# Two integers spread over the partitions by a stream shuffle instead of a matmul, and one row of 17 dummies

## Chip, cores and metric

One core of a Trainium2 chip. The time is device microseconds (us) from the start of the program to its end, the median of several runs. A few microseconds at the start of the program are what the change touches; the span of the whole is over 600 us.

## What is computed

Attention with a band and a few global keys, then two feed-forward layers. `n_global` and `n_local` are 64-bit integers that are known only at run time.

```python
def _attn_ref(q, k, v, n_global, n_local):          # q, k, v: 2 x 8 x 768 x 64
    scores = scale * np.matmul(q, k.transpose(0, 1, 3, 2))
    rel = pos[:, None] - pos[None, :]
    is_global = pos[None, :] < int(n_global)
    is_local = (rel >= 0) & (rel < int(n_local))
    keep = is_global | is_local
    dist = np.where(is_global & ~is_local, float(n_local), np.abs(rel))
    scores = np.where(keep, scores - slopes[:, None, None] * dist, -1e9)
    a = np.exp(scores - np.max(scores, axis=-1, keepdims=True))
    a = a / (np.sum(a, axis=-1, keepdims=True) + 1e-09)
    return np.matmul(a, v)

def reference(...):
    x = attention, as 1536 x 512
    h = x @ w1_in;  x = np.maximum(0.01 * h, h) @ w1_out          # 512 -> 2048 -> 512
    h = x @ w2_in;  return (P(h) / (Q(h) + 1e-06)) @ w2_out       # polynomials in h
```

## The kernel before

The program has three stages: attention for 8 pairs of heads (up to about 100 us), then the first and the second feed-forward layer, all bound by TensorE (PE). Products of large tiles are made of three passes over a high and a low part of each operand (`qh`, `ql`, `kh`, `kl`). Each engine runs its instructions in the order in which the code issues them; the order was written out by hand, with tables such as `BUSY`, `PREP` and `DECS` that say after which unit of work a piece goes out. The lines outside the hand-ordered part, the loading of the two integers among them, may be moved on their queue by the compiler of the program.

The start, with which the change deals, runs so:

- ACT's DMA queue loads the two integers into one partition of the tile `ints` (L95, L96), and after them one half of the first k block (`kr`, L300). SP's queue loads the rest: q's first half for both heads of pair 0, k's first half of the other head, then the second halves, then k, v and q of pair 1.
- VectorE (DVE) fills the tile `warm` with ones. PE then multiplies `warm` by itself into the tile `idle`: these are the dummies of `keep_busy(n)` (L489), whose result nobody reads. `BUSY = (14, 1, 3, 2, 1, 2)` is how many stand at each of six places.
- GpSimd (POOL) makes the identity (`ident`), and index tables with iotas; DVE makes the distances from them (`misc`, L236, L237, L239) and turns the integers into floats (`read_ints`, L106 to L109), which gives two numbers in one partition (`num1`).
- After 14 dummies, PE multiplies a row of ones by `num1` (L500), which puts the two numbers into all 128 partitions of a PSUM tile (`spread`), and then does one more dummy. DVE copies them to `nums` (L509).
- From `nums`, DVE makes the mask (L245, L248) and the first part of the bias (L251). The distances in `misc` and the bias are kept for the whole attention.
- Meanwhile PE transposes q's first half and k's first half (L331). ScalarE (ACT) rounds them to `qh` (L370) and `kh` (L341), and DVE makes the rests `ql` (L372) and `kl` (L343), on its queue behind L251. Then PE multiplies `kh` by `qh`, and, after a few dummies, `kl` by `qh` and `kh` by `ql` (L402).

From the products with `kl` on, PE has nearly always something to do. What later pieces need of q, k and v comes by SP's queue, 96 KB or 192 KB at a time in packets of 256 bytes.

Of the kernel before, what the change touches and what calls it, by code (L numbers as in the profile page):

```python
# [8 lines left out]
F32 = mybir.dt.float32  # L9
F32R = mybir.dt.float32r  # L10
I32 = mybir.dt.int32
U32 = mybir.dt.uint32
AF = mybir.ActivationFunctionType
ALU = mybir.AluOpType
# [3 lines left out]
P = 128  # L18
# [8 lines left out]
def attention_moe_moe2(  # L27
# [15 lines left out]
    nc = tc.nc  # L43
# [17 lines left out]
    LOAD_Q = 5  # L61
    XOUT = (8, 9)

    BUSY = (14, 1, 3, 2, 1, 2)

    FIRST = 8
    XOUT_LAST = (1, 8)
# [17 lines left out]
    RUN_AHEAD = 2  # L85

    W2 = 2 * P
    BW = W2 + P

    cpool = ctx.enter_context(tc.tile_pool(name="cpool", bufs=1))  # L90
    xpool = ctx.enter_context(tc.tile_pool(name="xpool", bufs=1))


    ints = cpool.tile([1, 4], I32, name="ints")
    nc.scalar.dma_start(ints[:, 0:2], n_local.bitcast(I32).partition_broadcast(1))  # L95
    nc.scalar.dma_start(ints[:, 2:4], n_global.bitcast(I32).partition_broadcast(1))  # L96
    intf = cpool.tile([1, 4], F32, name="intf")
    num1 = cpool.tile([1, 2], F32, name="num1")
    warm = cpool.tile([P, P], F32R, name="warm")
    ones = warm.bitcast(F32)[0:1]  # L100
    nums = cpool.tile([P, 2], F32, name="nums")
    n_loc = nums[:, 0:1]
    n_glo = nums[:, 1:2]

    def read_ints():
        nc.vector.tensor_copy(intf, ints)  # L106
        lo, hi = (intf.rearrange("p (j w) -> p j w", w=2)[:, :, w] for w in range(2))
        nc.vector.scalar_tensor_tensor(hi, lo, 0.0, hi, ALU.is_lt, ALU.add)
        nc.vector.scalar_tensor_tensor(num1, hi, 4294967296.0, lo, ALU.mult, ALU.add)  # L109

    coef = cpool.tile([P, 8], F32, name="coef")

# [110 lines left out]
    def window_bias(bpool, rpool):  # L223
# [6 lines left out]
        mask = misc2[:, 0:BW]  # L230
        nc.gpsimd.iota(rel_i[:, 0:W2], [[-1, W2]], base=P, channel_multiplier=1)
        nc.gpsimd.iota(rel_i[:, W2:BW], [[-1, P]], base=0, channel_multiplier=1)
        col_i = bpool.tile([P, GW], I32, name="col_i")
# [10 lines left out]
        def far():  # L244
            nc.vector.tensor_scalar(mask, dist, n_loc, FAR, ALU.is_ge, ALU.mult)  # L245
            mask_g = misc2[:, 0 : 2 * W2].rearrange("p (a c) -> p a c", a=2)[:, :, 0:GW]
            col_g = col.unsqueeze(1).to_broadcast([P, 2, GW])
# [10 lines left out]
    def attention(wpool, w1, ffn):  # L258
        with ExitStack() as actx:
# [4 lines left out]
            ps = actx.enter_context(tc.tile_pool(name="ps", bufs=2, space=PSUM))  # L264
# [4 lines left out]
            def blocks(t, s):  # L269

                if s == 0:
                    return t[:, 0 : HB * W2].rearrange("p (i c) -> p i c", c=W2)[:, :, 0:P]
                c0 = HB * W2 - P
# [213 lines left out]
            def keep_busy(n, rows=P):  # L487
                for _ in range(n):
                    nc.tensor.matmul(  # L489
                        idle[:, 0:W2].rearrange("p (a c) -> p a c", a=2),  # L490
                        warm[0:rows],
                        warm[0:rows].unsqueeze(1).to_broadcast([rows, 2, P]),
                        start=True,
                        stop=True,
                    )

            bias, bias_far, bias_near, bias_half = window_bias(bpool, rpool)
            keep_busy(BUSY[0])
            spread = ps.tile([P, W2], F32, tag="pt", name="spread")[:, 0:2]
            nc.tensor.matmul(spread, ones, num1, start=True, stop=True)  # L500
            keep_busy(BUSY[1])
            q0, k0, q1, k1 = P_[0].prep_q(0), P_[0].prep_k(0), P_[0].prep_q(1), P_[0].prep_k(1)
            next(q0)
            next(k0)
            next(q0)
            next(k0)
            keep_busy(BUSY[2])
            own, rest = slice(W2, BW), slice(0, W2)
            nc.vector.tensor_copy(nums, spread)  # L509
            bias_far()  # L510
            bias_near(own)
            next(q0, None)
# [102 lines left out]
            while n < len(U) or running or n <= len(U) + LV + 1:  # L615

                for m in GROUPS.get(n, ()):
                    for step, _ in enumerate(zip(unit(m).scores(), unit(m + 1).scores())):
                        if n == 0 and step == 0:
                            keep_busy(BUSY[3], P // 2)  # L620
                    if m == 2:
                        for _ in zip(unit(4).scores(), unit(5).scores()):
                            pass
                        keep_busy(BUSY[4])
                for m in LEASTS.get(n, ()):
                    unit(m).least()
                    if m == 1:
                        bias_near(rest)
                        bias_half(rest)
                if unit(n - 1) and n != 3:  # L630
                    unit(n - 1).exp()
                if unit(n - 3):
                    unit(n - 3).transposes()
                    if n == 4:
                        keep_busy(BUSY[5], P // 2)
                    unit(n - 3).evacuate()
                if n == 3:
                    unit(2).exp()
                for m in {LV: (), LV + 1: (0, 1)}.get(n, (n - LV,)):
                    if unit(m):  # L640
                        unit(m).values()
                if unit(n - LV - 1) and unit(n - LV - 1).ih == HB - 1 and unit(n - LV - 1).j == 1:
                    unit(n - LV - 1).finish()
                fillers(n)
                n += 1
# [516 lines left out]
```

## Time and profile before

| | us |
|---|---|
| median of 3 runs | 634.55 (634.18 to 634.83) |
| the profiled execution, its time | 633.84 |
| its span | 632.1 |
| PE busy in the span | 625.4 (99%) |
| DVE, ACT, POOL busy | 468.5, 437.0, 208.7 |

The span is the time from the first to the last instruction of the trace; the 1.7 us between it and the profiled execution's time lie around it. In the chain of work that ended last, 99% of the span is PE's. To read such a kernel: where PE is always busy, its instructions follow each other and their sum is the time; only where PE waits can another engine's work change the end. PE's idle time is in the first microseconds and at the end. The page's column for the granted clock shows the full level in every slice; for the very start, the durations of the dummies have to be looked at beside it.

### The profile page before, as it was taken

The page shows a single profiled execution, that of the slowest core. Times are in us where ns is not written, and L with a number is a line of the kernel's source. Part 1 is how long each engine was busy: PE and PEld are TensorE (multiplying, and loading weights), DVE is VectorE, ACT ScalarE, POOL GpSimd, SP SyncE. Part 2 cuts the span into 40 slices and gives each one's busy share as a digit, 9 for nine tenths or more (in the row PEclk, how much of TensorE's full clock was granted, in tenths as well). Part 3 has the DMA queues.
Part 4 walks back from the last instruction along what each step waited for, and adds up shares of the span by engine and source line. Part 5 has one row for each costly group of instructions (what it writes and reads, how often), then busy time and mean ns, then how long its engine had stood idle before and what let it go on. Part 6 is the DMA issues. An engine that isn't in the chain of part 4 may idle for free.

```text
span 632.1 us, 9657 instructions
## 1 busy us (share of the span) xinstructions
PE 625.4 (99%) x3289; PEld 527.2 (83%) x3289; DVE 468.5 (74%) x931; ACT 437.0 (69%) x828; POOL 208.7 (33%) x223
## 2 busy tenths in 40 slices
PE   9999999999999999999999999999999999999996
PEld 7999998888888888888888888888888888888885
DVE  7889887878887555456444489998777777897785
ACT  5899997868866455455344477876677888876673
POOL 4888864534443334341000012222222222112220
PEclk9999999999999999999999999999999999999999
DMA  9998643854367776764332200000033331100002
GB/s 190 225 181 177 153 114 109 278 197 167 99 194 236 225 242 195 238 194 177 100 100 94 92 16 34 1 1 1 0 104 97 100 95 46 63 33 0 2 1 73
DMA packets 80895, 73.34 MB, mean 116 GB/s; under 512 B 50948, under 2 KB 67332, under 8 KB 80836
## 3 DMA queue, kind: packets, MB, share of 16 engines
q1 hardware_dynamic: 79920, 71.09, 39.5%
q0 software_dynamic: 224, 0.92, 0.4%
q8 instruction: 28, 0.46, 0.3%
q10 hardware_dynamic: 692, 0.62, 0.3%
q14 instruction: 31, 0.25, 0.1%
HBM read 60.69 MB, written 11.93 MB: 115 GB/s over the span
## 4 chain that ended last, share of the span: by engine, by line
PE 99%; DVE 0%; issue 0%
PE h L675 41%; PE y L798 21%; PE y L796 21%; PE pt L438 4%; PE sc L402 3%; PE o L460 3%; PE o L459 2%; PE h L331 2%; PE h L211 1%; PE idle L489 1%; PE o L457 0%; DVE ot L814 0%; PE xt L211 0%; PE spread L500 0%; DVE kl L343 0%; DVE ql L372 0%
## 5 line engine op out<-in xcount | busy, mean ns | idle before, releaser
L675 PE MATMUL h<-xh,w 128*128 128x512 f32 x768 | 253.5, 390 | 0.0
L675 PEld LDWEIGHTS h<-xh,w 128*128 128x128 f32 x768 | 144.3, 188 | 29.8
L675 PE MATMUL h<-xl,w 128*128 128x512 f32 x384 | 149.6, 389 | 0.0
L731 POOL TENSOR_TENSOR gl<-u,gh 128x512 fp32r<-128x512 f32 x44 | 57.1, 1298 | 264.6 <-PE y L798 125.6
L796 PE MATMUL y<-gh,w 128*128 128x512 f32 x384 | 126.1, 389 | 0.0
L798 PE MATMUL y<-w,gh 128*128 128x512 f32 x384 | 125.7, 390 | 0.0
L166 POOL TENSOR_TENSOR dec<-dec,wraw 128x512 int32<-128x512 int32 x48 | 64.1, 1344 | 82.5 <-DVE wraw L153 79.2
L798 PEld LDWEIGHTS y<-w,gh 128*128 128x128 f32 x384 | 72.0, 188 | 15.1 <-ACT gh L910 0.3
L796 PEld LDWEIGHTS y<-gh,w 128*128 128x128 f32 x384 | 72.1, 188 | 15.0
L675 PEld LDWEIGHTS h<-xl,w 128*128 128x128 f32 x384 | 72.1, 188 | 14.5
L798 PE MATMUL y<-w,gl 128*128 128x512 f32 x192 | 75.1, 391 | 0.0
L796 PE MATMUL y<-gl,w 128*128 128x512 f32 x192 | 74.7, 389 | 0.0
L700 DVE TENSOR_TENSOR gl<-h,gh 128x512 fp32r<-128x512 f32 x48 | 33.0, 688 | 52.4 <-ACT gh L699 52.4
L699 ACT ACTIVATE gh<-h 128x512 fp32r<-128x512 f32 x48 | 28.6, 596 | 59.7 <-PE y L796 56.4
L750 ACT ACTIVATE h<-h 128x512 f32<-128x512 f32 x48 | 28.7, 597 | 52.8 <-PE h L675 52.6
L695 DVE SCALAR_TENSOR_TENSOR h<-h,g 128x512 f32<-128x512 f32 x48 | 33.3, 694 | 25.8 <-ACT g L694 25.7
L737 DVE SCALAR_TENSOR_TENSOR w<-w,epsq,h 128x512 f32<-128x512 f32 (+1 forms) x49 | 36.6, 747 | 20.6 <-ACT h L761 19.9
L694 ACT ACTIVATE g<-h 128x512 f32<-128x512 f32 x48 | 28.7, 598 | 29.8 <-PE h L675 29.8
L752 DVE SCALAR_TENSOR_TENSOR w<-h,coef,w 128x512 f32<-128x512 f32 x48 | 36.0, 749 | 16.1 <-ACT w L751 16.0
L427 ACT ACTIVATE pr<-sn,st 128x256 f32<-128x256 f32 (+1 forms) x96 | 47.1, 495 | 0.2 <-DVE st L413 0.2
L798 PEld LDWEIGHTS y<-w,gl 128*128 128x128 f32 x192 | 36.1, 188 | 8.5 <-POOL gl L731 1.1
L796 PEld LDWEIGHTS y<-gl,w 128*128 128x128 f32 x192 | 36.0, 188 | 7.4
(124 smaller groups left out, 1117.3 us busy)
## 6 DMA issues: line engine op xcount, KB each, us to landing
wraw<-in_moe_w_in_dram SPq DMA_DIRECT2D x24, 512.0 KB, 4.5
wraw<-in_moe_w_out_dram SPq DMA_DIRECT2D x24, 512.0 KB, 4.8
scratch<-dec SPq DMA_DIRECT2D x32, 256.0 KB, 5.5
wf<-scratch SPq DMA_DIRECT2D x16, 512.0 KB, 3.5
w<-in_moe_w_in_dram SPq DMA_DIRECT2D x8, 512.0 KB, 4.4
w<-in_moe_w_out_dram SPq DMA_DIRECT2D x8, 512.0 KB, 5.3
vc<-in_v_dram SPq DMA_DIRECT2D x16, 192.0 KB, 3.4
qkraw<-in_q_dram SPq DMA_DIRECT2D x6, 512.0 KB, 3.5
```

Source lines behind the costliest of these rows:

```text
L166: nc.gpsimd.tensor_tensor(ti, ti, self.c, ALU.add)
L427: nc.scalar.activation(self.pr[:, :w], self.sn[:, :w], AF.Exp, bias=self.least_at, scale=-1.0,)
L675: nc.tensor.matmul(h, wt[:, m, c * P : (c + 1) * P], xs[:, c, cs], start=c == 0 and n == 0, stop=c == NK - 1 and n == 2,)
L694: nc.scalar.activation(g, h, AF.Copy)
L695: nc.vector.scalar_tensor_tensor(h, h, 0.01, g, ALU.mult, ALU.max)
L700: nc.vector.tensor_tensor(gl, h, gh.bitcast(F32), ALU.subtract)
L731: (nc.gpsimd if on_pool else nc.vector).tensor_tensor(gl, g, gh.bitcast(F32), ALU.subtract)
L737: yield nc.vector.scalar_tensor_tensor(ow, ow, epsq, oh2, ALU.add, ALU.mult)
L750: nc.scalar.activation(h2, h, AF.Square)
L752: nc.vector.scalar_tensor_tensor(w0, h2, coef[:, 7:8], w0, ALU.mult, ALU.add)
L796: nc.tensor.matmul(ys[d], wt[:, m, ds_], gs, start=st, stop=sp)
L798: nc.tensor.matmul(ys[d], gs[:, ds_], wt[:, m, :], start=st, stop=sp)
```

## The change

The two integers now go into partitions 0, 32, 64 and 96 of a tile of 128 partitions, which POOL has filled with zeros. A stream shuffle of DVE copies, in each group of 32 partitions, the first one's row to all 32 (a list of 32 zeros says from which partition each takes its row). The conversion to floats then runs on all partitions and writes `nums` at once. PE's multiplication by ones, the PSUM tile and DVE's copy are gone, and the 14 dummies and the one behind the multiplication become 17 in a row. The other places keep their number of dummies.

```diff
-    BUSY = (14, 1, 3, 2, 1, 2)
+    BUSY = (17, 3, 2, 1, 2)
...
+    QUAD = 32
...
-    ints = cpool.tile([1, 4], I32, name="ints")
-    nc.scalar.dma_start(ints[:, 0:2], n_local.bitcast(I32).partition_broadcast(1))
-    nc.scalar.dma_start(ints[:, 2:4], n_global.bitcast(I32).partition_broadcast(1))
-    intf = cpool.tile([1, 4], F32, name="intf")
-    num1 = cpool.tile([1, 2], F32, name="num1")
+    ints = cpool.tile([P, 4], I32, name="ints")
+    nc.gpsimd.memset(ints, 0)
+    nc.scalar.dma_start(ints[0:P:QUAD, 0:2], n_local.bitcast(I32).partition_broadcast(P // QUAD))
+    nc.scalar.dma_start(ints[0:P:QUAD, 2:4], n_global.bitcast(I32).partition_broadcast(P // QUAD))
+    spread = cpool.tile([P, 4], I32, name="spread")
+    intf = cpool.tile([P, 4], F32, name="intf")
...
     def read_ints():
-        nc.vector.tensor_copy(intf, ints)
+        nc.vector.stream_shuffle(spread, ints, [0] * QUAD)
+        nc.vector.tensor_copy(intf, spread)
         lo, hi = (intf.rearrange("p (j w) -> p j w", w=2)[:, :, w] for w in range(2))
         nc.vector.scalar_tensor_tensor(hi, lo, 0.0, hi, ALU.is_lt, ALU.add)
-        nc.vector.scalar_tensor_tensor(num1, hi, 4294967296.0, lo, ALU.mult, ALU.add)
+        nc.vector.scalar_tensor_tensor(nums, hi, 4294967296.0, lo, ALU.mult, ALU.add)
...
             keep_busy(BUSY[0])
-            spread = ps.tile([P, W2], F32, tag="pt", name="spread")[:, 0:2]
-            nc.tensor.matmul(spread, ones, num1, start=True, stop=True)
-            keep_busy(BUSY[1])
...
-            keep_busy(BUSY[2])
+            keep_busy(BUSY[1])
             own, rest = slice(W2, BW), slice(0, W2)
-            nc.vector.tensor_copy(nums, spread)
```

On PE, at the start of the program, stands before (`idle` is the dummies' tile, `h` the bank that takes transposes, `sc_133` and `sc_134` the banks of the scores):

```order
L489 MATMUL idle<-warm 128x256 x14
L500 MATMUL spread<-num_65,warm 128x2
L489 MATMUL idle<-warm 128x256
L331 MATMUL h<-ident,qr 128x128 x3
L331 MATMUL h<-ident,kr 128x128 x3
L489 MATMUL idle<-warm 128x256 x3
```

and now, two lines lower in the file:

```order
L491 MATMUL idle<-warm 128x256 x17
L333 MATMUL h<-ident,qr 128x128 x3
L333 MATMUL h<-ident,kr 128x128 x3
L491 MATMUL idle<-warm 128x256 x3
L404 MATMUL sc_134<-kh,qh 128x128
```

The transposes of q now stand directly behind the dummies; the rest of PE's order is the same to the end.

On ACT, the start of its queue before:

```order
L95 DMA ints<-in_n_local_dram 1x2
L96 DMA ints<-in_n_global_dram 1x2
L300 DMA kr<-in_k_dram 128x3x64
L370 ACT_TABLE_LOAD
L370 ACTIVATE qh<-h 128x384
```

and now:

```order
L302 DMA kr<-in_k_dram 128x3x64
L97 DMA ints<-in_n_local_dram 4x2
L98 DMA ints<-in_n_global_dram 4x2
L372 ACT_TABLE_LOAD
L372 ACTIVATE qh<-h 128x384
```

The load of k, which stood behind the two integers, is now ahead of them; the first of the integers waits for POOL's zeros.

On DVE, from the reading of the integers to the rests of q and k, before:

```order
L106 CAST intf<-ints 1x4
L108 SCALAR_TENSOR_TENSOR intf<-intf 1x2
L109 SCALAR_TENSOR_TENSOR num_65<-intf 1x2
L239 TENSOR_TENSOR misc<-misc,misc_155 128x384
L241 CAST col<-col_i 128x32
L509 COPY nums<-spread 128x2
L245 TENSOR_SCALAR misc_155<-misc,nums 128x384
L248 SCALAR_TENSOR_TENSOR misc_155<-col,nums,misc_155 128x2x32
L251 SCALAR_TENSOR_TENSOR bias<-misc,nums,misc_155 128x128
L372 SCALAR_TENSOR_TENSOR ql<-h,qh 128x384
```

and now:

```order
L107 STREAM_SHUFFLE spread<-ints 128x4
L108 CAST intf<-spread 128x4
L110 SCALAR_TENSOR_TENSOR intf<-intf 128x2
L111 SCALAR_TENSOR_TENSOR nums<-intf 128x2
L241 TENSOR_TENSOR misc<-misc,misc_156 128x384
L243 CAST col<-col_i 128x32
L247 TENSOR_SCALAR misc_156<-misc,nums 128x384
L250 SCALAR_TENSOR_TENSOR misc_156<-col,nums,misc_156 128x2x32
L253 SCALAR_TENSOR_TENSOR bias<-misc,nums,misc_156 128x128
L374 SCALAR_TENSOR_TENSOR ql<-h,qh 128x384
```

One instruction came in ahead of the cast and the copy behind `col` went; nothing between the integers and the bias waits for PE any more. On POOL the filling with zeros came in as the first instruction of the kernel. SP's queue is the same.

## Rows read from the trace of the kernel before

**Rows 1.** The page, the chain of work that ended last, by engine

```profile
PE 99%; DVE 0%; issue 0%
```

**Rows 2.** Stretches: PE, PEld, DVE, ACT, POOL busy; then granted clock, DMA share, GB/s

```profile
4.50:5.00 0.50, 0.50 (x3) 0.48 (x4) 0.06 (x1) 0.00 (x0) 0.00 (x0) 1.00 0.77 175
12.00:14.00 2.00, 2.00 (x21) 1.83 (x23) 1.92 (x8) 1.46 (x4) 1.23 (x3) 1.00 1.39 206
20.00:100.00 80.00, 79.87 (x800) 75.39 (x800) 69.85 (x275) 73.07 (x190) 61.38 (x87) 1.00 0.76 167
100.00:620.00 520.00, 520.00 (x2311) 430.26 (x2311) 378.64 (x583) 348.60 (x604) 135.71 (x106) 1.00 0.33 106
```

**Rows 3.** The chain that ended last, in order of time: start, us, what

```profile
6.73 0.48 DVE kl L343
...
7.25 0.44 PE sc L402 x4
7.69 0.81 PE h L331 x6
```

**Rows 4.** PE's weight loads in order of time: start us, us, instruction

```profile
1.05 3.06 PEld L489 LDWEIGHTS idle<-warm 128*128 128x128 f32 x14 [1.05 <-DVE epsq L203]
4.33 0.49 PEld L500 LDWEIGHTS spread<-num,warm 1*128 1x128 f32 x2 [0.22 <-issue]
4.83 0.19 PEld L489 LDWEIGHTS idle<-warm 128*128 128x128 f32 x1
4.97 0.35 PEld L331 LDWEIGHTS h<-ident,qr 128*128 128x128 f32 x3
...
5.61 0.42 PEld L489 LDWEIGHTS idle<-warm 128*128 128x128 f32 x3
```

**Rows 5.** The dummies' line: durations in ns (least, median, most), first and last start

```profile
L489 PEld LDWEIGHTS idle<-warm x23: 183/330/333, 1.0 to 10.0; 128*128 128x128 f32 x19, 64*128 64x128 f32 x4
```

**Rows 6.** DVE in order of time

```profile
2.92 0.15 DVE L106 CAST intf<-ints 1x4 f32<-1x4 int32 x1
3.10 0.15 DVE L108 SCALAR_TENSOR_TENSOR intf<-intf 1x2 f32<-1x2 f32 x1
...
3.36 0.54 DVE L239 TENSOR_TENSOR misc<-misc,misc 128x384 f32<-128x384 f32 x1
3.83 0.16 DVE L241 CAST col<-col_i 128x32 f32<-128x32 int32 x1
4.94 0.16 DVE L509 COPY nums<-spread 128x2 f32<-128x2 f32 x1 [0.95 <-PE spread L500]
5.14 0.42 DVE L245 TENSOR_SCALAR misc<-misc,nums 128x384 f32<-128x384 f32 x1
...
6.18 0.55 DVE L372 SCALAR_TENSOR_TENSOR ql<-h,qh 128x384 fp32r<-128x384 f32 x1
```

**Rows 7.** ACT and POOL in order of time (ACTq: ACT's DMA issues)

```profile
0.73 0.53 ACTq L95 DMA_DIRECT2D ints<-in_n_local_dram  x1
...
0.87 0.12 POOL L284 MEMSET vc<- 128x12 f32 x1
...
1.30 0.23 ACTq L96 DMA_DIRECT2D ints<-in_n_global_dram  x1
...
1.56 0.41 ACTq L300 DMA_DIRECT2D kr<-in_k_dram  x1
...
5.59 0.49 ACT L370 ACTIVATE qh<-h 128x384 fp32r<-128x384 f32 x1 [2.31 <-PE h L331]
```

**Rows 8.** DMA issues, pair 0's k and pair 1's q: KB each, us to landing

```profile
kr<-in_k_dram ACTq DMA_DIRECT2D x1, 96.0 KB, 2.5
...
qr<-in_q_dram SPq DMA_DIRECT2D x1, 192.0 KB, 4.6
```

**Rows 9.** Order of time: SP's issue of pair 1's q, PE's first use

```profile
8.36 0.67 SPq L300 DMA_DIRECT2D qr<-in_q_dram  x1
...
13.11 0.31 PEld L331 LDWEIGHTS h<-ident,qr 128*128 128x128 f32 x3
```

More of the change, by code (lines that the diff above doesn't have):

```diff
@@ L91, in attention_moe_moe2 @@
     xpool = ctx.enter_context(tc.tile_pool(name="xpool", bufs=1))
-    ints = cpool.tile([1, 4], I32, name="ints")
-    nc.scalar.dma_start(ints[:, 0:2], n_local.bitcast(I32).partition_broadcast(1))
-    nc.scalar.dma_start(ints[:, 2:4], n_global.bitcast(I32).partition_broadcast(1))
-    intf = cpool.tile([1, 4], F32, name="intf")
-    num1 = cpool.tile([1, 2], F32, name="num1")
+    ints = cpool.tile([P, 4], I32, name="ints")
[4 more added lines that the diff above has]
+    intf = cpool.tile([P, 4], F32, name="intf")
     warm = cpool.tile([P, P], F32R, name="warm")
-    ones = warm.bitcast(F32)[0:1]
     nums = cpool.tile([P, 2], F32, name="nums")
@@ L619, in attention @@
                         if n == 0 and step == 0:
-                            keep_busy(BUSY[3], P // 2)
+                            keep_busy(BUSY[2], P // 2)
                     if m == 2:
@@ L623, in attention @@
                             pass
-                        keep_busy(BUSY[4])
+                        keep_busy(BUSY[3])
                 for m in LEASTS.get(n, ()):
@@ L634, in attention @@
                     if n == 4:
-                        keep_busy(BUSY[5], P // 2)
+                        keep_busy(BUSY[4], P // 2)
                     unit(n - 3).evacuate()
```

## Prediction, made before the run

> **What bounds the kernel now.** I read the page's chain first: 99% of the span is PE's [rows 1]. Then the stretches: from 20 to 100 us PE is busy for 79.87 of 80.00 us, from 100 to 620 us for all of 520.00 [rows 2]. So nothing that the change does to DVE, ACT or POOL later on can count, and whatever PE's dense run gains or loses at its start is carried to the end, unless PE then meets a wait that it now just misses. The chain in order of time says where the dense run starts: up to 7.25 us the last to arrive is DVE with `kl`, from there on PE's own instructions follow each other [rows 3]. The question is when PE can start its products with `kl`, now 7.25 us, and whether it then has its data.
>
> **PE's side of the start.** The weight loads show two paces. The 14 dummies' loads take 3.06 us, the last of them 0.33 (the median) [rows 4, 5], so one dummy comes each (3.06 - 0.33) / 13 = 0.21 us. The three dummies at 5.61 us take 0.42 us, the last of them about 0.19, so one comes each 0.11 to 0.12 us [rows 4]. That is the engine's clock at 1.2 GHz and at 2.4 GHz, though the column for the granted clock shows 1.00 already in the early stretch [rows 2]. Between them lie the two passes of the spreading matmul, still slow (0.49 us), and the single dummy at 4.83 us, fast (0.19 us) [rows 4]: the level rose somewhere from 4.33 to 4.83 us, after PE had worked without a break since 1.05 us, but for 0.22 us.
>
> Removed from PE: the spreading matmul and the dummy behind it, which take the queue from 4.33 to 4.97 us, where q's transposes begin, 0.64 us. Added there: three dummies. At the slow pace they cost 3 x 0.21 = 0.63 us and q's transposes begin at 4.96 us, no gain; at the fast pace 3 x 0.11 = 0.33 us, they begin at 4.66 us, a gain of 0.31. The rise lies in this very stretch; I take two slow and one fast, 0.53 us, so 4.86 us and a **gain of 0.11 us**. ACT's `qh`, which waits for these transposes [rows 7], moves along, and so does `kh` behind it.
>
> **DVE's side of the start.** Now `qh` ends at 5.59 + 0.49 = 6.08 us [rows 7], yet `ql` starts at 6.18 us [rows 6]: DVE was still at the bias, because its copy of `nums` had waited 0.95 us for PE. So DVE costs 0.10 us today. In the changed kernel `nums` needs no PE. What the row from the integers to `ql` takes: the shuffle, which no row here shows; nearest are the cast of the integers and the copy it replaces, 0.15 and 0.16 us, and the next starts 0.18 us after the first (2.92 to 3.10); the widest it could be is like a pass over 128x384, 0.54. I take 0.18, since only four columns pass. Then cast and two conversions as now, 2.92 to 3.36 = 0.44; L239, 0.47; `col` and the changeover 0.20 (as from the copy at 4.94 to L245 at 5.14); L245 to `ql`, 6.18 - 5.14 = 1.04 [rows 6]. The sum is 2.33 us, 2.7 with the widest shuffle.
>
> When can it start? The second integer is now issued at 1.30 us and the cast that needs it starts at 2.92 us, so it lands within 1.62 us [rows 6, 7]. In the changed kernel k's load goes first on ACT's queue; the integers' places are then 1.30 and 1.56 us, if an issue takes what it takes now. The second lands 1.62 us later, at 3.18 us, or at the latest like k's own load from that place, 2.5 us later, at 4.06 us [rows 8]. So `ql` can have DVE at 3.18 + 2.33 = 5.51 us, at the latest at 6.39 us. `qh` ends at 6.08 - 0.11 = 5.97 us. I take the near value: DVE is ready 0.46 us early, `ql` starts when `qh` is there, and the 0.10 us are **gained** too.
>
> Beside the path: POOL's zeros cost about 0.12 us, the first integer's load waits for them until some 0.9 us and is only due at 1.30 [rows 7]; the identity and the index tables behind them come as much later, and PE reaches the identity only after 17 dummies, DVE waits for the integers longer. Were that cover gone, they would cost their 0.12. PE's other dummies keep their number.
>
> **The sum.** 0.11 + 0.10 = 0.21 us earlier at `kl` and so at the products at 7.25. What is late next: pair 1's q. Its second load is issued at 8.36 us and lands 4.6 us later, at 12.96 [rows 8, 9]; PE wants it at 13.11 us. If the transfers stay where they are, PE can come at most some 0.1 us earlier there, and half the gain is lost. But k's load starts 1.56 - 0.73 = 0.83 us earlier (0.73 is ACT's first place [rows 7]), and the DMA engines had room in this time: their share is 0.77 in the stretch at 4.5 us against 1.39 from 12 us on [rows 2]. So I expect the transfers, too, to come forward by some tenths, and the gain to be kept. The Trainium skill ("DMA: Bandwidth & Descriptors", "Issuing engines are not separate DMA queues") says that transfers issued by several engines run on the same 16 DMA engines and interleave, so that a second issuer saves only the time of the issue. By that rule, 12.96 would stay and the sum be 0.1 instead of 0.21.
>
> The profiled execution's 633.84 us becomes 633.63. It lies 0.71 us under the median of the runs; on the median's side the forecast is 634.55 - 0.2 = 634.35.
>
> **The rivals.**
> A. *The integers come late and DVE is the bound.* For it: they now stand behind k's 384 packets on ACT's queue. If the second lands at 4.06 us, `ql` starts at 6.39 us, 0.21 later than now, with the wide shuffle 0.6 later: 634.75 to 635.15. Break-even is a landing at 6.18 - 2.33 = 3.85 us. Against it: the integers are a few bytes and now need under 1.62 us. The skill's page on DMA ("Two DMAs through the same engine are not ordered") has descriptors of one queue start in order, which speaks for the late value; no row shows the landing behind a large load.
> B. *Pair 1's q holds PE back.* The gain is cut at 13.0 us to about 0.1, or to nothing: 634.45 to 634.55. For it, the 0.15 us between landing and use; against it, the room on the DMA engines.
> C. *The clock stays low longer.* Slower. If the level of 2.4 GHz came only after the first products instead of before the transposes, PE's part of the path would run at half pace: q's and k's transposes (six, 0.81 us like those at 7.69), the four products (0.44) and the next six transposes (0.81) [rows 3], 2.06 us more, less the 0.2 gained: 636.4. It decides the sign beyond my limit when some 1.5 us of these 2.06 are doubled. Against it: PE now has more of the same dummies in a row and no 0.22 us break.
> D. *All three dummies run fast.* 0.31 + 0.10 = 0.41 us: 634.15. Needs the rise by 4.2 us.
> E. *The change doesn't do what it says*, the shuffle waits for something of PE after all: DVE's order shows no such wait. It would be 0.0 to 0.1, like B.
>
> More than D can hardly be won: 14 x 0.21 + 3 x 0.11 us of dummies keep PE until 4.3 us even with a fast end, and q's transposes begin at 4.97 now.
>
> **How the numbers follow.** Forecast 0.45, A 0.22, B and E 0.17, D 0.10, C 0.06. A measurement of this kernel can tell about 0.2% from no change, 1.27 us. The forecast, A, B, D and E all lie within that; only C does not, 0.05 of its 0.06. I leave 0.02 for a gain over 1.27 us, at the far end of D with a shift in the runs. So faster 0.02, same 0.93, slower 0.05. The three runs spread by 0.65 us, and a median taken another time may lie as far off; so the range goes from D less that, 634.15 - 0.65 = 633.5, to the near A and that, 634.75 + 0.65 = 635.4, which holds the far A too. C is left out.
>
> **What would show it.** In the trace after: q's transposes begin near 4.86 us; the shuffle starts near 3.2 us and takes about 0.15; `ql` starts right when `qh` ends, near 5.97; the products with `kl` near 7.04; pair 1's q lands by 12.9, and PE's transposes of it begin near 12.9. From then on all PE instructions keep their distance. Wrong would be: a shuffle after 3.85 us, DVE idle in front of it and `ql` behind `qh` (A); PE waiting for q at 13.0 (B); weight loads of 0.33 us after 4.97 (C).

## The result, and the profile after

| | us |
|---|---|
| before | 634.42 median of 10 runs (633.82 to 634.83) |
| changed | 638.73 median of 10 runs (635.82 to 641.48) |
| ratio | 1.0069, interval 1.0052 to 1.0086 |
| forecast | 634.35 (633.5 to 635.4) |

The changed kernel is slower by 4.3 us, 0.7%, and the forecast of no change was wrong. Two things stand out beside the median. The runs spread over 5.7 us, those of before over 1.0. And they are ordered by TensorE's mean granted clock: the fastest, 635.82 us, has 0.999, those at 637 have 0.996, the slowest, at 641.4, 0.987. The profiled execution took 636.89 us with a span of 635.1; before, it was 633.84 and 632.1.

The page of the changed kernel, PE's busy tenths and the granted clock in 40 slices, and the chain that ended last by engine:

```profile
PE   8999999999999999999999999999999999999996
...
PEclk8999999999999999999999999999999999999999
...
PE 98%; DVE 1%; DMA 0%; POOL 0%; issue 0%; POOLq 0%; ACTq 0%; DVEq 0%
```

PE still sets the time, but against [rows 1] DVE and a DMA have come into the chain, and the first slice of the clock is no longer full. The chain in order of time (start, us, what) says which DMA:

```profile
2.42 2.54 DMA ints<-in_n_global_dram
```

The second integer is issued at 2.42 us and lands at 4.96. ACT's queue in order of time (ACTq is a DMA issue) shows why so late:

```profile
0.73 0.52 ACTq L302 DMA_DIRECT2D kr<-in_k_dram  x1
1.29 1.10 ACTq L97 DMA_DIRECT2D ints<-in_n_local_dram  x1
2.42 0.51 ACTq L98 DMA_DIRECT2D ints<-in_n_global_dram  x1
```

Against [rows 7], the integers stand behind k, and their issues take 1.10 and 0.51 us instead of 0.53 and 0.23. DVE in order of time:

```profile
5.06 0.01 DVE L107 LOAD_MASK_SELECT spread<-ints  x1 [2.03 <-DMA ints<-in_n_global_dram]
5.09 0.16 DVE L107 STREAM_SHUFFLE spread<-ints 128x4 int32<-128x4 int32 x1
5.29 0.17 DVE L108 CAST intf<-spread 128x4 f32<-128x4 int32 x1
...
6.81 0.65 DVE L250 SCALAR_TENSOR_TENSOR misc<-col,nums,misc 128x64 f32<-128x64 f32 x1
...
7.76 0.55 DVE L374 SCALAR_TENSOR_TENSOR ql<-h,qh 128x384 fp32r<-128x384 f32 x1
8.22 0.55 DVE L345 TENSOR_TENSOR kl<-h,kh 128x384 fp32r<-128x384 f32 x1
```

DVE stands idle for 2.03 us in front of the shuffle, and casts at 5.29 us where it cast at 2.92 [rows 6]. `ql` starts at 7.76 instead of 6.18, `kl` at 8.22 us, where the row of the kernel before is

```profile
6.65 0.55 DVE L343 TENSOR_TENSOR kl<-h,kh 128x384 fp32r<-128x384 f32 x1
```

PE's weight loads in order of time, after the change:

```profile
1.05 3.70 PEld L491 LDWEIGHTS idle<-warm 128*128 128x128 f32 x17 [1.05 <-DVE epsq L205]
4.69 0.59 PEld L333 LDWEIGHTS h<-ident,qr 128*128 128x128 f32 x3
5.27 0.60 PEld L333 LDWEIGHTS h<-ident,kr 128*128 128x128 f32 x3
5.83 0.42 PEld L491 LDWEIGHTS idle<-warm 128*128 128x128 f32 x3
...
8.83 0.18 PEld L404 LDWEIGHTS sc<-kl,qh 64*128 64x128 f32 x2 [1.74 <-DVE kl L345]
8.93 0.19 PEld L404 LDWEIGHTS sc<-kh,ql 64*128 64x128 f32 x2
9.20 0.50 PEld L333 LDWEIGHTS h<-ident,kr 128*128 128x128 f32 x3
9.68 0.66 PEld L333 LDWEIGHTS h<-ident,qr 128*128 128x128 f32 x3
```

q's transposes begin at 4.69 us, earlier than before (4.97 [rows 4]), but they run at the slow pace: their loads take 0.59 us instead of 0.35. The level of 2.4 GHz, there by 4.83 us before, comes between 5.27 and 5.83 us here; the dummies at 5.83 take 0.42 us as they did before. The column for the granted clock shows nothing of this first rise, and it is not what holds PE up next, since DVE is later still. PE waits 1.74 us for `kl`, and the products with `kl` come at 8.83 instead of 7.25 us [rows 3], 1.58 later. And something else happens there: the three loads of a transpose at 9.20 and 9.68 us take 0.50 and 0.66 us, though the ones at 8.93 were still quick. The stretches (PE, PEld, DVE, ACT, POOL busy, then the granted clock, DMA share, GB/s):

```profile
7.00:9.10 2.10, 0.56 (x8) 0.36 (x5) 1.87 (x5) 0.29 (x1) 0.68 (x2) 1.00 1.29 233
9.10:12.60 3.50, 3.50 (x23) 2.87 (x22) 2.00 (x8) 1.99 (x6) 1.48 (x4) 0.51 1.37 213
12.60:20.00 7.40, 7.40 (x70) 6.50 (x70) 6.49 (x29) 6.00 (x16) 4.11 (x7) 1.00 1.38 209
100.00:620.00 520.00, 520.00 (x2323) 430.64 (x2322) 378.53 (x589) 349.34 (x606) 135.95 (x105) 1.00 0.33 107
```

From 9.1 to 12.6 us the granted clock is 0.51: TensorE runs at 1.2 GHz, right after it was busy for only 0.56 of 2.10 us. In 3.5 us at half the clock it does about 1.75 us less, by estimate. The sum is 1.58 + 1.75 = 3.3 us; the profiled executions differ by 3.05. From 12.6 us on the level is full, and PE's dense run is what it was [rows 2].

So there are two questions: what makes the integers late, and what makes the clock fall.

### The profile page after: what moved, and what is told of

Read it like the earlier page. It is cut to its first block, busy times and chain, and to the rows that moved or that the text cites. A ratio compares the mean times of both kernels' runs of the same rounds, so it can differ in the third digit from the quotient of the medians.

```text
span 635.1 us, 9659 instructions
## 1 busy us (share of the span) xinstructions
PE 627.1 (99%) x3289; PEld 529.0 (83%) x3289; DVE 469.7 (74%) x932; ACT 437.3 (69%) x828; POOL 208.6 (33%) x224
## 4 chain that ended last, share of the span: by engine, by line
PE 98%; DVE 1%; DMA 0%; POOL 0%; issue 0%; POOLq 0%; ACTq 0%; DVEq 0%
PE h L673 41%; PE y L796 21%; PE y L794 21%; PE pt L440 4%; PE sc L404 4%; PE o L462 3%; PE o L461 2%; PE h L333 2%; PE h L213 1%; PE o L459 0%; DMA ints<-in_n_global_dram 0%; PE idle L491 0%; DVE ot L812 0%; PE xt L213 0%; DVE misc L250 0%
```

## The experiments

Of the first, two theories: the load into **four places** is slow by itself (theory F in the expectations), or the **place behind k** on ACT's queue is what delays it (theory Q). Of the second: the level falls because PE has a **gap** while it waits for `kl` (theory G), or it is only the late DVE that costs, in some other way. The times of before in the runs below are 634.34, 634.44, 634.5 and 634.29 us in the four groups of kernels that ran together (23 of its runs for the third, 14 for the last, over 30 for the others).

### What makes the integers late

**e1_ints_first.** The changed kernel with the integers' loads written in the hand-ordered part, ahead of k:

```diff
+            nc.scalar.dma_start(ints[0:P:QUAD, 0:2], n_local.bitcast(I32).partition_broadcast(P // QUAD))
+            nc.scalar.dma_start(ints[0:P:QUAD, 2:4], n_global.bitcast(I32).partition_broadcast(P // QUAD))
             (the loads of pair 0, k's on ACT among them)
```

> The changed kernel, with the loads of the two integers put ahead of k's load on ACT's queue, as in the kernel before; zeros, four partitions, shuffle and 17 dummies stay. Theory Q (the place in ACT's queue): behind k's 96 KB the integers land near 5.0 us; ahead of it they land by about 3.2 us, the shuffle starts by 3.3 us, the rests of q near 6.0, the products with the low part of k near 7.0, PE never stands still long enough to lose its level of 2.4 GHz; median 634.2 to 634.6, runs within 1 us. Theory F (a load into four partitions is slow by itself, its issue took 1.10 us against 0.23 to 0.53): the shuffle still starts after 4.3 us, median over 636, spread over 2 us.

Measured: 634.63 us (634.41 to 636.07), ratio 1.0007 (0.9998 to 1.0016): no difference from before. ACT's queue, then DVE's wait:

```profile
0.86 1.12 ACTq L481 DMA_DIRECT2D ints<-in_n_local_dram  x1
2.02 0.58 ACTq L482 DMA_DIRECT2D ints<-in_n_global_dram  x1
2.63 0.46 ACTq L300 DMA_DIRECT2D kr<-in_k_dram  x1
```

```profile
4.47 0.01 DVE L105 LOAD_MASK_SELECT spread<-ints  x1 [1.44 <-DMA ints<-in_n_global_dram]
```

Neither theory's forecast came true as a whole: the shuffle is as late as F said, the median is near Q's. Two of the 11 runs lie at 636.0 to 636.1, with a granted clock of 0.996 and 0.997. With this place alone the loss is gone in the median, but the integers are still late: with nothing in front, the shuffle comes at 4.50 us, 1.6 later than the cast of before, and the products at 7.88. The loads into four places take as long to issue as behind k. And k, now last, becomes late itself: PE waits 0.56 us for it at 5.84 us.

**e2_before_k_first.** The kernel before, its loads into one partition moved behind k's:

```diff
-    nc.scalar.dma_start(ints[:, 0:2], n_local.bitcast(I32).partition_broadcast(1))
-    nc.scalar.dma_start(ints[:, 2:4], n_global.bitcast(I32).partition_broadcast(1))
...
             (the loads of pair 0, k's on ACT among them)
+            nc.scalar.dma_start(ints[:, 0:2], n_local.bitcast(I32).partition_broadcast(1))
+            nc.scalar.dma_start(ints[:, 2:4], n_global.bitcast(I32).partition_broadcast(1))
```

> The kernel before (matmul that spreads, one partition), with only the integers' loads moved behind k's load on ACT's queue. Theory Q: the integers land near 4 to 5 us instead of by 2.9, the spreading matmul and with it q's transposes wait on PE's queue, median 635.5 to 639 with a spread of several us. Theory F: one partition stays quick, median 634.4 like before, within 0.5.

Measured: 635.09 us (634.04 to 641.86), ratio 1.0027 (1.0005 to 1.0048). Eight runs lie at 634.0 to 635.2, four at 638.8 to 641.9; the profiled execution is the slowest, 641.86. DVE:

```profile
4.26 0.16 DVE L104 CAST intf<-ints 1x4 f32<-1x4 int32 x1 [1.26 <-DMA ints<-in_n_global_dram]
```

**e5_before_four_places.** The kernel before, its loads at their old place, but into four partitions; DVE reads only the first. No zeros, no shuffle:

```diff
-    ints = cpool.tile([1, 4], I32, name="ints")
-    nc.scalar.dma_start(ints[:, 0:2], n_local.bitcast(I32).partition_broadcast(1))
+    ints = cpool.tile([P, 4], I32, name="ints")
+    nc.scalar.dma_start(ints[0:P:32, 0:2], n_local.bitcast(I32).partition_broadcast(4))
     (n_global likewise)
...
-        nc.vector.tensor_copy(intf, ints)
+        nc.vector.tensor_copy(intf, ints[0:1])
```

> The kernel before, its integers loaded first on ACT's queue as there, but each into four partitions (0, 32, 64, 96) instead of one; the spreading matmul reads partition 0 as before, no zeros, no shuffle. Theory F (four places cost issue time by themselves): the first issue takes about 1.1 us instead of 0.53, the second about 0.55 instead of 0.23, the cast on DVE starts at 3.9 to 4.4 us instead of 2.92, and the spreading matmul waits for it: q's transposes at 5.3 to 5.6 instead of 4.97, median 634.6 to 635.5 or more if the level of 2.4 GHz is touched. Theory Q alone (only the place in the queue counts): issues 0.5 and 0.25 us, cast by 3.1, median as before, 634.3.

Measured: 636.95 us (634.29 to 639.09), ratio 1.0038 (1.0021 to 1.0055). ACT's queue and DVE:

```profile
0.74 1.12 ACTq L95 DMA_DIRECT2D ints<-in_n_local_dram  x1
1.90 0.51 ACTq L96 DMA_DIRECT2D ints<-in_n_global_dram  x1
```

```profile
4.26 0.16 DVE L106 CAST intf<-ints 1x4 f32<-1x4 int32 x1 [1.27 <-DMA ints<-in_n_global_dram]
```

With these two, the 2 x 2 is complete. When DVE gets the integers:

| | ahead of k | behind k |
|---|---|---|
| one place | 2.92 us (before) | 4.26 us (e2) |
| four places | 4.26 us (e5) | 5.09 us (changed) |

Both theories are right: each alone costs DVE 1.34 us, both together 2.17. In e5 the second issue starts 0.60 us later than in the kernel before (1.90 against 1.30), the other 0.74 us lie between the issue and the landing. (In the kernel before DVE did not wait for the integers, so they may have landed before 2.92.)

Both kernels lost time though their integers came before those of e1: in them PE's own matmul still spreads the numbers, so their lateness stops PE ahead of q's transposes, which begin at 5.58 us instead of 4.97. In the profiled executions (636.58 and 641.86 us) these 0.61 us are the smaller part of the loss. PE's weight loads in e5, then two rows of e2:

```profile
4.84 0.50 PEld L500 LDWEIGHTS spread<-num,warm 1*128 1x128 f32 x2 [0.73 <-DVE num L109]
...
5.58 0.59 PEld L331 LDWEIGHTS h<-ident,qr 128*128 128x128 f32 x3
...
11.55 0.33 PEld L402 LDWEIGHTS sc<-kh,ql 64*128 64x128 f32 x2
12.07 0.19 PEld L489 LDWEIGHTS idle<-warm 128*128 128x128 f32 x1 [0.19 <-issue]
```

```profile
22.81 0.55 PEld L457 LDWEIGHTS o<-vp,pts 128*128 128x128 f32 x2
...
24.11 0.30 PEld L457 LDWEIGHTS o<-vp,pts 128*128 128x128 f32 x2
```

In both, PE waits 0.73 us in front of the spreading matmul, where it was 0.22 [rows 4], and in these executions the slow pace, over by 4.83 us in the kernel before, lasts until about 12 us in e5 and 23 us in e2. That is a level that rises late, the mechanism of rival C. The mean granted clock doesn't tell it (0.998 to 1.0 in all runs of both kernels); only the durations of the loads do. That the longer wait is what delays the rise is likely, but not shown; and what the level does in their shorter runs no trace shows.

**e6_all_places.** The changed kernel with loads into all 128 partitions, ahead of k; no zeros, no shuffle:

```diff
-    nc.gpsimd.memset(ints, 0)
-    nc.scalar.dma_start(ints[0:P:QUAD, 0:2], n_local.bitcast(I32).partition_broadcast(P // QUAD))
+    nc.scalar.dma_start(ints[:, 0:2], n_local.bitcast(I32).partition_broadcast(P))
     (n_global likewise)
...
-        nc.vector.stream_shuffle(spread, ints, [0] * QUAD)
-        nc.vector.tensor_copy(intf, spread)
+        nc.vector.tensor_copy(intf, ints)
```

> The changed kernel with each integer loaded straight into all 128 partitions, so that no zeros and no shuffle are needed and the loads stay ahead of k's on ACT's queue. If the issue time grows with the places (0.53 for one, 1.1 for four): over 1.5 us, worse than the changed kernel, median over 637. If it is the step between the partitions (32 apart) that is slow, not their number: issue about 0.5 us, the cast by 3.3 us, products with the low part of k near 7.0, median 634.0 to 634.4.

Measured: 635.01 us (634.7 to 639.98), ratio 1.0028 (1.001 to 1.0045). ACT's queue and DVE:

```profile
0.73 0.43 ACTq L96 DMA_DIRECT2D ints<-in_n_local_dram  x1
1.20 0.45 ACTq L97 DMA_DIRECT2D ints<-in_n_global_dram  x1
```

```profile
4.95 0.17 DVE L105 CAST intf<-ints 128x4 f32<-128x4 int32 x1 [1.96 <-DMA ints<-in_n_global_dram]
```

Neither of the two forecasts came true. The issue is quick, quicker than that of four places, so it is not the number of places that makes those slow to issue; whether it is the step of 32 between them no run shows. But the landing takes 3.7 us from the issue, and q and k behind the many small pieces are late too: PE waited 0.84 us in front of q's transposes (5.33 us). How long an issue takes does not tell when its data are there.

**e8_no_load.** The changed kernel without the two loads: POOL writes the values as constants. It leaves out the reading of the integers, and measures what the rest of the change is worth when they are never late:

```diff
-    nc.gpsimd.memset(ints, 0)
-    (the two loads)
+    for c, n in enumerate((96, 0, 8, 0)):
+        nc.gpsimd.memset(ints[:, c : c + 1], n)
```

> The changed kernel without the loads of the two integers: their values are written as constants into the tile, which then goes through the same shuffle and conversion. It leaves out the two loads, so its time is that of the change if the integers came in time. The prediction's other terms stand alone here: shuffle 0.15 to 0.18 us near 3.1 us, q's transposes at 4.66 to 4.96, the rests of q right when qh ends (near 5.9), products with the low part of k near 7.0 instead of 7.25, pair 1's q landing before 13.0, median 634.0 to 634.4 (0.1 to 0.4 under before). Rival (17 dummies in a row or the shuffle do harm by themselves, or the earlier k load crowds the DMA engines): median over 634.6.

Measured: 634.22 us (633.93 to 634.71), ratio 0.9998 (0.9989 to 1.0006). DVE:

```profile
3.04 0.15 DVE L106 STREAM_SHUFFLE spread<-ints 128x4 int32<-128x4 int32 x1
...
6.25 0.56 DVE L373 SCALAR_TENSOR_TENSOR ql<-h,qh 128x384 fp32r<-128x384 f32 x1 [0.83 <-ACT qh L371]
```

Here the integers are in time, as the forecast had it: the shuffle comes near 3 us, DVE is ready 0.83 us before `qh`, and the time is 634.22 us where 634.35 was forecast. But the way there is another. PE's weight loads:

```profile
4.69 0.59 PEld L332 LDWEIGHTS h<-ident,qr 128*128 128x128 f32 x3
...
7.49 0.19 PEld L403 LDWEIGHTS sc<-kl,qh 64*128 64x128 f32 x2 [0.19 <-DVE kl L344]
```

The transposes run at the slow pace, `ql` starts at 6.25 instead of 5.97 us, and the products with `kl` come at 7.49, not at 7.04 as forecast and later than the 7.25 of the trace of before.

**e11_four_shuffles.** The changed kernel with neither cause: the integers go into one partition, ahead of k, and four shuffles from there fill the four groups of 32:

```diff
-    ints = cpool.tile([P, 4], I32, name="ints")
+    ints = cpool.tile([QUAD, 4], I32, name="ints")
-    (the two loads)
...
-        nc.vector.stream_shuffle(spread, ints, [0] * QUAD)
+        for r in range(0, P, QUAD):
+            nc.vector.stream_shuffle(spread[r : r + QUAD], ints, [0] * QUAD)
...
+            nc.scalar.dma_start(ints[0:1, 0:2], n_local.bitcast(I32).partition_broadcast(1))
+            nc.scalar.dma_start(ints[0:1, 2:4], n_global.bitcast(I32).partition_broadcast(1))
             (the loads of pair 0, k's on ACT among them)
```

> The changed kernel, in which the integers go into one partition only, by loads that stand ahead of k's on ACT's queue as in the kernel before, and four shuffles of 32 x 4 from that partition's group of 32 fill the four groups. It takes away both causes found for the late integers (the load into four places, 1.3 us; the place behind k, 1.3 us) and pays three more shuffles. If these are the causes: the first shuffle at 2.9 to 3.1 us, four of them 0.15 to 0.18 each, the cast near 3.6, ql near 5.9 to 6.2, and a median of 634.1 to 634.5 (e8, without the loads: 634.22). If a load that waits for POOL's zeros, or a shuffle from one group of 32 to another, costs by itself: the cast at 4.0 us or later and 634.6 to 635.5.

Measured: 634.51 us (634.14 to 634.68), ratio 1.0000 (0.9991 to 1.0009). DVE's first shuffle, the cast and `ql`:

```profile
3.04 0.15 DVE L106 STREAM_SHUFFLE spread<-ints 32x4 int32<-32x4 int32 x1
...
3.73 0.17 DVE L107 CAST intf<-spread 128x4 f32<-128x4 int32 x1
...
6.24 0.56 DVE L373 SCALAR_TENSOR_TENSOR ql<-h,qh 128x384 fp32r<-128x384 f32 x1 [0.32 <-ACT qh L371]
```

The shuffle waits for nothing, four of them end 0.7 us after the first started, and DVE still waits for `qh`; as in e8, the transposes are slow and the products come at 7.49 us. The 4.3 us are back, to within the interval of 0.6 us. So the way of the two integers by DMA was the whole cause, and the shuffle itself is harmless.

### What makes the clock fall

**e4_more_dummies.** The changed kernel with 16 dummies instead of 2 in front of the products with `kl`, where PE waits:

```diff
-    BUSY = (17, 3, 2, 1, 2)
+    BUSY = (17, 3, 16, 1, 2)
```

> The changed kernel, with 16 instead of 2 dummies of 64 rows where PE waits for the low part of k (from 6.84 us on, about 0.12 us each, until 8.7). The integers stay late. Theory G (PE's idle time lets the level fall to 1.2 GHz, after PE is working again): PE is busy in the wait, the level stays at 2.4, only the late DVE is left: median 635.6 to 636.2, runs within 1 us, products with the low part of k at 8.8. Rival (the level falls for another reason, or it is not the level that spreads the runs): median 638 to 639, spread over 4 us.

Measured: 635.87 us (635.5 to 636.29), ratio 1.0023 (1.0014 to 1.0031). The same loads, integers as late as ever (the shuffle at 5.22 us, the products at 9.19, still after a wait for `kl`), but the spread is gone and 2.9 us with it: no run is above 636.29, where nine of the ten of the changed kernel are. The stretches:

```profile
7.00:9.00 2.00, 1.57 (x14) 1.36 (x12) 1.93 (x6) 0.00 (x0) 0.28 (x1) 1.00 1.29 230
9.00:13.00 4.00, 3.81 (x34) 3.14 (x35) 3.56 (x18) 3.27 (x10) 1.48 (x4) 1.00 1.40 206
```

PE is busy for 1.57 us of the 2.00 in front, not 0.56 of 2.10, and the level stays at 2.4 GHz. The loss of 4.3 us thus falls into about 635.87 - 634.34 = 1.5 us of late DVE and 638.73 - 635.87 = 2.9 us of clock.

**e10_before_late_dve.** The test from the other side: the kernel before, with its loads, dummies and matmul, in which DVE makes the mask five times instead of once:

```diff
-            nc.vector.tensor_scalar(mask, dist, n_loc, FAR, ALU.is_ge, ALU.mult)
+            for _ in range(5):
+                nc.vector.tensor_scalar(mask, dist, n_loc, FAR, ALU.is_ge, ALU.mult)
```

> The kernel before, in which DVE makes the mask (the pass of 0.42 us behind the copy of the two numbers) five times instead of once; the four repeats change nothing in the result. kl and the products with kl come 1.6 to 1.8 us later, near 8.9 us, like the changed kernel's 8.83, while loads, dummies and the way of the integers stay as before. If the lateness of kl alone makes PE's level fall (theory G): a median of 636 to 640, with runs that spread by 2 us or more, and weight loads of the transposes at the slow pace after 9 us. If the fall has to do with the changed kernel's loads, shuffle or dummies: 634.4 + 1.6 = 636.0, within 0.5 us.

Measured: 639.57 us (637.48 to 640.23, 6 runs), ratio 1.0073 (1.0058 to 1.0089). The wait of PE, and the stretches:

```profile
9.44 0.19 PEld L403 LDWEIGHTS sc<-kl,qh 64*128 64x128 f32 x2 [1.74 <-DVE kl L344]
```

```profile
7.00:10.50 3.50, 1.96 (x16) 1.40 (x15) 3.04 (x11) 1.11 (x4) 0.97 (x2) 1.00 1.35 215
10.50:17.30 6.80, 6.80 (x36) 5.30 (x35) 3.56 (x14) 4.22 (x12) 2.44 (x6) 0.50 1.40 211
```

None of the change is in this kernel, and it shows the same picture: PE waits 1.74 us for `kl`, runs on at 2.4 GHz for a microsecond, and then at 1.2 GHz, here for 6.8 us. The products are 9.44 - 7.25 = 2.2 us late, more than the 1.6 to 1.8 expected, mainly because L249 behind the repeats took 0.64 us instead of 0.28; the median is 5.1 later. The late `kl` alone is enough: 2.2 us of it cost about three more at the clock here, and e4 shows that work in the gap saves them. Theory G holds so far.

**e3_read_later.** The changed kernel, with `read_ints()` behind the two passes of DVE that don't need the integers:

```diff
-        read_ints()
         nc.vector.tensor_tensor(dist, dist, mask, ALU.add)
         col = bpool.tile([P, GW], F32, name="col")
         nc.vector.tensor_copy(col, col_i)
+        read_ints()
```

> The changed kernel, with DVE's two passes that need no integers (the sum of distances and mask, the index column) put ahead of the shuffle instead of behind the conversions. The integers land as late as now (near 5.0 us). Theory: what is queued behind the wait costs 0.47 + 0.12 us on the path, and the pass over 64 columns would no longer run beside POOL's copies of k (0.65 us instead of 0.28): products with the low part of k at 7.9 to 8.3 us instead of 8.83, median 635.0 to 636.5, fewer falls of the level. Rival (DVE's order is covered, only the landing counts): products at 8.8, median as the changed kernel, 638 to 639.

Measured: 635.02 us (634.75 to 641.24), ratio 1.0025 (1.0006 to 1.0044). DVE does some 0.65 us of work (3.07 to 3.72) while it waits, and the products come at 8.47 instead of 8.83 us. Ten of the twelve runs lie at 634.75 to 635.28, two at 639.63 and 641.24.

**e7_read_later_dummies.** The same with 12 dummies in front of the products:

```diff
-    BUSY = (17, 3, 2, 1, 2)
+    BUSY = (17, 3, 12, 1, 2)
     (and read_ints() as in e3_read_later)
```

> The kernel with DVE's two passes ahead of the shuffle, and besides 12 instead of 2 dummies of 64 rows where PE waits for the low part of k. Without the dummies 2 of 12 runs were at 639.6 and 641.2, the others at 634.75 to 635.3. Theory G (the level of 2.4 GHz is lost in PE's idle time): no run over 636, the rest unchanged at 634.8 to 635.3. Rival (another cause of the slow runs): again runs over 638.

Measured: 635.21 us (635.02 to 635.49), ratio 1.0013 (1.0004 to 1.0021). No run is above 635.49: the two disturbed ones of e3 don't come (none of 11 against 2 of 12 could be chance by itself; with e4 it fits), and the others lie at 635.2 against e3's 634.9. Against e4, the order of DVE's passes is worth 635.87 - 635.21 = 0.66 us.

One thing stays open. In e3's profiled run PE had a longer gap than in the changed kernel (1.91 us against 1.74), and the level did not fall:

```profile
8.47 0.19 PEld L404 LDWEIGHTS sc<-kl,qh 64*128 64x128 f32 x2 [1.91 <-DVE kl L345]
...
8.84 0.31 PEld L333 LDWEIGHTS h<-ident,kr 128*128 128x128 f32 x3
```

A gap makes the fall possible, it does not settle it. The first rise varies as well, behind the same 17 dummies from 1.05 us on: in e3 it is there for q's transposes at 4.61 us (0.35 us), in the changed kernel only behind 5.27, in e11 not yet for the three dummies at 5.90 (0.76 us). The Trainium skill ("TensorE: Matmul & The Clock Gate", Part 1) says that the gate looks at the engine's activity in a rhythm of its own, which does not begin with the kernel, so that the same kernel can be caught or not; that would fit a rise at different times and runs of one kernel that differ by 5 us, but no run here shows the rhythm.

### Can the start be won at all?

**e9_no_load_14.** e8_no_load with 14 dummies in the row instead of 17 (`BUSY = (14, 3, 2, 1, 2)`), again with constants in place of the integers.

> The changed kernel with the integers' values as constants (it leaves out the two loads, and is right for these integers alone), as e8_no_load, but with 14 dummies in the row instead of 17. It measures what the three added dummies do when DVE is early. If they only take PE's time (0.11 to 0.21 us each): q's transposes begin 0.3 to 0.6 us earlier, near 4.1 to 4.4 us, if q has landed by then; qh comes with them and the median is 633.9 (e8: 634.22). If they are needed for the level of 2.4 GHz: the level rises later or falls again, the runs spread, and the median is 634.5 to 637. If q lands only near 4.7 us, as the transposes of the kernel before don't tell: no difference from e8, 634.2.

Measured: 634.36 us (634.01 to 634.64), ratio 0.9999 (0.9990 to 1.0007). q's transposes begin at 4.11 us, the products with `kl` at 6.68 instead of e8's 7.49, but:

```profile
13.24 0.31 PEld L332 LDWEIGHTS h<-ident,qr 128*128 128x128 f32 x3 [0.62 <-issue]
```

PE reaches pair 1's q and waits there (0.5 us for the DMA in the table of waits). In e8 the same load starts at 13.62 us: of 0.81 us at the products, 0.38 are left, and the medians don't tell the two apart.

**e12_q_sooner.** e11_four_shuffles with 14 dummies, and pair 1's q loaded ahead of pair 0's second v block:

```diff
-    BUSY = (17, 3, 2, 1, 2)
+    BUSY = (14, 3, 2, 1, 2)
...
-            P_[0].load_vc(1)
             P_[1].load_q()
+            P_[0].load_vc(1)
```

> e11_four_shuffles with 14 dummies in the row instead of 17, and with pair 1's q loaded one place earlier on SP's queue, ahead of the second v block of pair 0. In e9_no_load_14 q's transposes began 0.58 us earlier (4.11 us) and PE then waited 0.5 us for pair 1's q. If that q is what held the gain back: q lands 0.4 us earlier, near 13.1 us, PE has nearly no idle time in front of it, and the median is 633.9 to 634.1, the best so far (before: 634.5). If the earlier start is lost elsewhere (the v block now late, another load that PE waits for): 634.3 to 634.8, no difference from the kernel before.

Measured: 635.31 us (634.82 to 636.86), ratio 1.0024 (1.0015 to 1.0034), slower. PE:

```profile
13.46 0.30 PEld L458 LDWEIGHTS o<-vc,pts 128*128 128x128 f32 x2 [1.48 <-DMA vc<-in_v_dram]
```

The v block that q overtook is now what PE waits for, 1.48 us. Four of the ten runs lie at 636.5 to 636.9 with a granted clock of 0.995 to 0.996, the others at 634.8 to 635.5 with 0.998 or more. In this order of loads an earlier start is lost again at the next one, and none of these versions beats the kernel before.

## Why the prediction was wrong

**The step that failed** is "When can it start?", and with it the price that rival A put on a late start. The step put the integers at 3.18 us, like now but 0.26 later, and held 4.06 to be the latest. They landed at 4.96. Two things that I had as one value each went wrong together:

- *The issue.* "If an issue takes what it takes now" put the first integer at 1.30 us, which was right (1.29), and the second 0.26 us behind it, at 1.56. It was issued 1.13 us behind it, at 2.42. Even [rows 7] have 0.57 us between the issues of the two integers (0.73 and 1.30); the rest is the four places. A load into four partitions, 32 apart, was nowhere in the trace of before, and I gave it the price of a load into one. That four places cost an issue more is shown by e5, where nothing else differs.
- *The landing.* From the issue it took 2.54 us (2.42 to 4.96), where I took 1.62. The bound of 2.5 us, from k's own load, was right; adding it to the wrong place gave 4.06.

With the issue where it was measured, the same bound reads 2.42 + 2.5 = 4.9 us. Even from the rows of before alone it would have been 1.30 + 0.57 + 2.5 = 4.37, past the break-even of 3.85. Rival A was right in its mechanism and had 0.22; its price, 0.2 to 0.6 us, was too small.

**The row from the integers to `ql`** was 2.33 us by the sum and 2.67 as measured (5.09 to 7.76). The shuffle was not at fault: the cast starts 0.20 us behind it, where I took 0.18. The difference is one pass, L250, with 0.65 us instead of 0.28. It started 0.10 us after POOL's additions to `kh` (L361, from 6.71 us on); in e1, where these came at 7.00 us, the pass was over by then and took 0.28 us. In e4 the `col` cast, 0.16 to 0.18 us elsewhere, took 0.65 when it started 0.06 us after them. The Trainium skill ("SBUF — State Buffer", section "SBUF: two separate sides") says that a pass of DVE with two operands in SBUF and one of POOL that reads SBUF lock each other out; the row of L250 agrees, and `ql` and `kl`, which read PSUM for one operand and in the kernel before ran beside the same work of POOL (from 6.54 us on), took 0.55 us there as here. No run takes POOL's work away, so this cause is argued and not shown. I had not asked what a later DVE would run into.

**The clock.** Rival C thought of a level that rises late, through PE's own dummies. In the traced execution it did rise late, between 5.27 and 5.83 us, but the later `kl` hid it. What cost time was something that I had left out: a wait can bring the level down again. I priced DVE's lateness in A as its microseconds alone; by e4 it cost 1.5 us so and 2.9 more at the clock, and in e10 2.2 us of lateness cost 5.1. The range's upper end, 635.4, came from A without this; the changed kernel's median lies 3.3 us above it. A and a loss of clock came together, and I had them as separate cases.

**What held, and what held by luck.** q's transposes were forecast at 4.86 us, 4.66 to 4.96, and begin at 4.69. That is luck. All 17 dummies ran at the slow pace ((3.70 - 0.33) / 16 = 0.21 us each), and for that the sum said 4.96. It had counted from 4.33 us, behind PE's wait of 0.22 us for the spreading matmul [rows 4], and this wait went with the matmul. The level was not up for the transposes, as the forecast needed. With the integers in time this decides: in e8 and e11 `ql` starts when `qh` is there, as forecast, but the products with `kl` come at 7.49 us instead of 7.04. So the 0.21 us of the sum were not won in these traces, and that their medians (634.22 and 634.51) lie near 634.35 is luck too; the intervals can't tell so little from nothing. The trace of before from which the sum was read, with its early rise, is one of the fastest executions (633.84; the median is 634.42).

POOL's zeros cost nothing that shows (0.10 us, and in e11 DVE does not wait for the integers behind them). Rival B held too: pair 1's q binds as soon as PE gains more than some tenths (e9). My hope that the transfers would come forward with k's earlier load was wrong: in the changed kernel k went out at 0.73 us, and SP's issue of pair 1's q still began at 8.01 us (7.77 before) and nothing of it was early. That is the rule of the Trainium skill that the prediction weighed ("DMA: Bandwidth & Descriptors", "Issuing engines are not separate DMA queues"), and the trace agrees with it. The sign of A that the prediction named, a shuffle after 3.85 us with DVE idle in front of it and `ql` behind `qh`, is what the trace shows.

## What to carry to other kernels

A small load is not free because it is small: where it stands on its queue, and into which places it goes, each moved it by 1.3 us here, both together by 2.2; issue and landing must be priced apart and added, and a shape of load that no row shows gets a wide bound. Look at which order the compiler gives a load that was made to wait for something (the zeros): it let k go first. And at a start where PE lives on dummies, a late operand costs twice: its own microseconds, and the clock that falls while PE waits; fourteen more dummies in front of the waiting product took 2.9 of 4.3 us away without touching the cause. For the level before its first change, read the durations of PE's loads, not the column for the clock: e2's profiled execution was slow for 23 us in a column that shows full.

## What the runs showed of the hardware that I had not expected

- The issue of a load of two integers on ACT's queue: 0.53 us (then 0.23 for the second) into one partition, 1.10 to 1.12 (then 0.51 to 0.58) into four that lie 32 apart, 0.43 (then 0.45) into all 128. The two issues of the last take about as long as those into one partition (0.88 us against 0.76), and its data land 3.7 us after the second.
- Two integers behind a load of 96 KB on the same queue reach DVE 1.34 us later than ahead of it (4.26 and 2.92 us), though their second issue comes only 0.61 us later (1.91 and 1.30).
- TensorE's level fell to 1.2 GHz not in PE's wait of 1.74 us but after it: 0.3 us behind its end in the changed kernel (8.83 us, slow from 9.1 on), some 1 us behind it in e10 (9.44, slow from 10.5 on). It stayed low for 3.5 and 6.8 us, though PE is shown as busy for all of these stretches.
- With a break of 0.73 us in front of the spreading matmul instead of 0.22, the first rise of the level came at about 12 us (e5) and 23 us (e2) instead of by 4.83, in one trace each, though PE is shown as busy for all of the time from 5 to 9 us in both (4.00 of 4.00 us).
- A shuffle of 128x4 integers takes 0.15 to 0.16 us, one of 32x4 into another group of 32 partitions 0.15; four in a row start 0.17 us apart. Its loading of the list shows as 0.01 us.
